# Attention, SoLU block and routed experts in one kernel: which queue issues the puts of p, the order of the last chunk's blocks, and the slots of three tails

## The chip, the cores and the metric

The kernel runs on one core of a Trainium2 chip (trn2). The metric is device microseconds for one execution. The kernel before takes 4489.14 us, the median of 3 runs (4488.82 to 4499.24).

## What is computed

Eight sequences of 3072 rows go through a squared-ReLU attention without softmax (its scores are `z zᵀ`, which is symmetric), then a SoLU block with a layer norm, then eight routed experts, one for each row. All matrix products are made at more than one pass' precision: each operand is split into a high and a low part, and three products are added.

```python
def _attn_ref(u, v, z):                      # u, v: (8, 3072, 256), z: (8, 3072, 64)
    scores = np.matmul(z, z.transpose(0, 2, 1)) / S
    attn = np.maximum(scores, 0.0) ** 2
    return u * np.matmul(attn, v)
def _moe_ref(x, w_in, w_out, g_ln):          # w_in: (256, 1024), w_out: (1024, 256)
    h = x @ w_in
    sm = softmax(h); solu = h * sm
    ln = (solu - mean(solu)) / sqrt(var(solu) + 1e-6) * g_ln
    return ln @ w_out
def _moe2_ref(x, w_gate, w1, w2):            # w1: (8, 256, 1024), w2: (8, 1024, 256)
    e = argmax(x @ w_gate); gate = softmax(x @ w_gate)[e]
    return gate * (np.maximum(x @ w1[e], 0.0) @ w2[e])
```

## The kernel before

**Chunks and slots.** The 24576 rows are cut into 48 chunks of 512 rows, six to a sequence; `c` counts chunks and j = c mod 6 is the place in the sequence. A chunk takes 24 slots, one for each block of 128 key rows. In a slot TensorE (PE) multiplies one block of squared scores `a`, split into `ah` and `al`, with that block's rows of v (`pe_av`: L108, L109, L110, two rounds of three matmuls into `o`). The order of everything is written out by hand: a loop over slots (L1044) emits for each slot the matmuls, what stands in a table of events (`at(slot, function, ...)`), and the steps of blocks that come up to seven slots later. Each engine and each queue runs its own list in this order, and nothing overtakes.

**Kept scores.** Since the scores are symmetric, a block that was made in an earlier chunk of the sequence is not made again. It is written to HBM (`put_out`, L399, `kept<-sym`) and read back (`get`, L406, `sym<-kept`, four transfers of 64 KB in runs of 128 bytes). `get` is emitted seven slots ahead of the block's own matmuls. Three slots behind `get` a block from four or more places back is transposed on VectorE (`turn_got`, L412); four slots behind it the block is split, the high part on ScalarE (`dve_hi`, L438), the low part a slot later on VectorE (`dve_lo`, L443). A chunk with j = 0, 1, 2, 3, 4, 5 reads 0, 4, 8, 12, 16, 16 of its 24 blocks; the rest needs two more matmuls (L422, L423) and two activations each. Only j up to 3 writes any.

**The tail of a chunk.** The 512 rows of chunk c then go through the SoLU block in four pieces t of 128 rows, six slots apart, while the slots of the next chunk run. For piece t the slot w = 24(c+1) + 2 + 6t counts: `blk_h` (PE), `blk_max` (DVE), `blk_exp` (ACT), `blk_mul` (DVE), at w + 4 `blk_turn` (a transposition on DVE into `pb`), at w + 5 `blk_put` (four transfers of 128 KB to HBM, `moved<-pb`, L536), later `blk_get` (four transfers back, `pT<-moved`, L542), `blk_split` (ACT and DVE) and `blk_y` (PE, then DVE into `y`). The four slot offsets of put, get, split and y are the tuple of L954. After the last piece come the scaling and the routing (mostly GpSimd, POOL) and four scatters of the rows into `sorted_rows` (`blk_scatter`, L659), one every two slots.

**Queues.** All transfers but the scatters are issued by SyncE's queue (SP), except that `blk_put` is issued by ScalarE's queue where its slot lies in a chunk with j = 4 or 5 and the tail is not the last one:

```python
at(w + out_, blk_put, c, t, nc.scalar if (w + out_) // NKB % NCB >= NCB - 2 and not last else nc.sync)
```

The program counts the transfers of SP and ScalarE on eight semaphores in turn (DMAHW0 to 7 in the rows of the order below), so that a transfer that comes to a semaphore is issued only after the transfer before it on that semaphore, eight back, has landed.

**The experts.** From slot NS = 1152 on, the sorted rows are taken in units of 512 rows (the first three in halves of 256), two matrix products each (`up`, `down`), while the tails of the chunks 45, 46 and 47 still run: their last scatters stand at NS + 8 to NS + 14, NS + 29 to NS + 35 and later. `load_x` (L805) reads a unit's rows out of `sorted_rows`; unit 2's stands at NS + 10. The tile `y` that a tail writes and its scatters read has two buffers, so chunk 47 writes the one that chunk 45 scattered from.

Of the kernel before, what the change touches and what calls it, by code (L numbers as in the profile page):

```python
# [33 lines left out]
def attention_moe_kernel(ctx, tc, u, v, z, w_in, w_out, g_ln, w_gate, w1, w2, out):  # L34
    nc = tc.nc
# [8 lines left out]
    NCB = S // CH  # L44
    NKB = S // P
    NCHUNK = B * NCB
# [6 lines left out]
    PD = 1  # L53
    ZL = 8
    XA, XT0, XE = 2, 21, 23
    SA, SB, SC, SD, SH = 11, 14, 16, 19, 1
    TW = 8
    WS, W0, W1, W2 = 4, -11, 0, 2
    YT = 1
# [72 lines left out]
    with ExitStack() as st:  # L132
# [22 lines left out]
        def at(slot, fn, *args):  # L155
            events[slot].append((fn, args))

        def after_them(slot, fn, *args):

            events_after[slot].append((fn, args))  # L160
# [3 lines left out]
        t = vp.tile([P, 2, 4, D], F32R, tag="vw", name="raw64").bitcast(I32).rearrange("p a r d -> p (a r d)")  # L164
        raw64 = [t[:, i * 2 * CH:(i + 1) * 2 * CH].rearrange("p (f two) -> p f two", two=2) for i in range(2)]
        t = mp.tile([P, F], F32, tag="pT", name="cu64").bitcast(I32)
        c64, u64 = t[:, :CH], t[:, CH:]
        t = [mp.tile([P, CH], F32R, tag=k, name="t64").bitcast(F32) for k in ("pth0", "ptl0", "pth1", "ptl1")]
# [165 lines left out]
        def again(q, k):  # L334
            return q == NCB - 2 and k == NCB - 1
# [11 lines left out]
        t = [xrow.tile([P, KD * CH], F32, tag="x", name="sym") for _ in range(2)]  # L347
        t = [x[:, i * CH:(i + 1) * CH] for x in t for i in range(2)]
# [3 lines left out]
        def order(j, end=False):  # L352


            old = [kb for kb in range(4 * j) if end or not again(kb // 4, j)]
            new = [kb for kb in range(NKB) if kb not in old]
            return [kb for _, kb in sorted([((i + 0.5) / len(old), kb) for i, kb in enumerate(old)] +
                                           [((i + 0.5) / len(new), kb) for i, kb in enumerate(new)])]

        orders = [order(c % NCB, c == NCHUNK - 1) for c in range(NCHUNK)]  # L360

        def block(n):
# [167 lines left out]

        moved = [nc.dram_tensor(f"moved_{i}", (32, 4, F), F32, kind="Internal").ap() for i in range(4)]

        def blk_put(c, t, eng):
            w = pb_t.pop((c, t))
            for x in range(4):
                eng.dma_start(out=moved[t][:, x], in_=w[x * 32:(x + 1) * 32])  # L536

        def blk_get(c, t):
            pT_t[c, t] = w = mp.tile([P, F], F32, tag="pT", name="pT")
# [299 lines left out]
        for i in range(NU):  # L839
            w = HALF if i < N_CUT else units[i]  # L840
# [71 lines left out]
        for c in range(NCHUNK):  # L912
            b, j = divmod(c, NCB)
            s0 = c * NKB
            sb = b * NCB * NKB
            if b == 0:
                base = 4 * j - Z0
                zload = base - 5 + (j > 0)
                vload = 4 * j - V0
                at(base, turn_z, c)  # L920
            else:

                late = j >= NCB - 2
                base = sb + 3 + 4 * (j - NCB + 2) if late else sb - (NCB - 1 - j) * NKB + ZB
                zload = base - (4 if late else ZL)
                vload = sb - NKB + VL + VS * j
                at(base - 2, turn_z, c)
            at(zload, load_z, c)
            at(base, prep_z, c)
            if c > 0:  # L930
                at(s0 - LA - 5, swap_z, c)
            for h in range(2):
                step, wait = (3, 5) if b else (2, 2)
                at(vload + step * h, load_v, c, h)
                at(vload + step * h + wait, prep_v, c, h)
                at(vload + step * h + wait + (b > 0), prep_v_lo, c, h)
            for x in range(4):
                at(s0 + 2 + x, load_u, c, x)
            at(s0 + 14, turn_u, c)

            last = c == NCHUNK - 1
            more = 2 if last else 1
            s1 = s0 + NKB
            for t in range(4):
                w = s1 + 2 + (TW if last else 6) * t
                at(w, blk_h, c, t, 0)
                at(w + 1, blk_h, c, t, 1)
                at(w + 1, blk_max, c, t)
                after_them(w + 2, blk_exp, c, t)
                at(w + 3, blk_mul, c, t)  # L950
                at(w + 4, blk_turn, c, t)
                at(w + 6, blk_var, c, t)

                out_, back, cut_, y = (4, 6, 10, 12) if last else (5, 8, 12, 15) if c < NCHUNK - 2 else (5, 7, 9, 12)  # L954

                at(w + out_, blk_put, c, t, nc.scalar if (w + out_) // NKB % NCB >= NCB - 2 and not last else nc.sync)
                at(w + back, blk_get, c, t)
                cut_, y = w + cut_, w + y
                at(cut_, blk_split, c, t, 0)
                at(cut_ + 1, blk_split, c, t, 1)  # L960
                at(y, blk_y, c, t, 0)
                at(y + 1, blk_y, c, t, 1)
            e = y + 3
            for i in range(3):
                at(e + more * i, blk_scale, c, i)
            for i in range(2):
                at(e + more * (3 + i), blk_scale, c, 3)
            at(e + more * 5, blk_logits, c)
            for i in range(10):
                at(e + more * (6 + i + 2 * (i > 5)), blk_route, c, i)  # L970
            for t in range(4):
                at(e + more * (6 + 2 * t), blk_rows, c, t)
                at(e + more * (18 + 2 * t), blk_scatter, c, t)
        after = e + more * 24
        for b in range(n_in + n_out):
            for i in range(14):
# [15 lines left out]
        s0 = NS - NKB  # L992
        at(s0, take, "raw1")
        at(s0, load_w, 0, 1)
        at(s0 + 5, take, "w1h")
        at(s0 + 10, take, "w1l")
        at(s0 + 14, take, "raw2")
        at(s0 + 14, load_w, 0, 2)
        at(s0 + 19, take, "xT0")
        at(NS, take, "w2h")  # L1000
        at(NS, take, "hT")
        at(NS, take, "w2l")
# [40 lines left out]
        with tc.manual_schedule():  # L1043
            for n in range(min(lo_slot, -LA), hi_slot + 1):  # L1044
                i = n + LA
# [62 lines left out]
```

## Time and profile before

| | us |
|---|---|
| median of 3 runs (lowest, highest) | 4489.14 (4488.82, 4499.24) |
| the profiled execution, its own time | 4495.23 |
| its span, first to last instruction | 4493.5 |
| PE busy in the span | 4293.5 (96%) |
| DVE, ACT, POOL busy | 3200.8, 2797.7, 1123.2 |
| granted TensorE clock, mean over the span | 0.981 |

The profiled execution lies 6.1 us above the median, and 1.7 us of its time lie outside of its span. The share of 96% is a mean over chunks that differ; the rows below take it apart by chunk.

### The profile page before, as it was taken

The numbers are of one execution on the slowest core, as the hardware profiler recorded it, in microseconds if no ns is written. First come the engines' busy times: TensorE is split into PE (matmuls) and PEld (weight loads), VectorE is DVE, ScalarE is ACT, GpSimd is POOL, SyncE is SP. The second block draws the span as 40 slices with busy tenths as digits, with TensorE's granted clock in tenths as the row PEclk, the third lists the DMA queues.
The fourth block names the chain that finished last, engine by engine and source line by source line (L and its number), as shares of the span: only waits on it lengthen the run. The fifth ranks groups of instructions, "written<-read, shape, count | busy, mean of one in ns | idle before, by whom it ended". The sixth has DMA issues, their size and how long they took to land. (4 is left out here: it accounts for less than half of the span.)

```text
span 4493.5 us, 74098 instructions
## 1 busy us (share of the span) xinstructions
PE 4293.5 (96%) x23458; PEld 3701.0 (82%) x23458; DVE 3200.8 (71%) x5624; ACT 2797.7 (62%) x5184; POOL 1123.2 (25%) x2358
## 2 busy tenths in 40 slices
PE   7999998999899999999999999999789999999998
PEld 5877887888788788878877887887678999999998
DVE  8767776777687677768767776777556755666686
ACT  6756775776577577658756765875444444444565
POOL 5022222322222232222223222322122211111112
PEclk9999999999999999999999999999889999999999
DMA  5887787778778778877887887778665655555575
GB/s 151 172 154 150 182 177 137 173 175 164 140 188 176 141 177 175 162 145 181 170 151 173 171 169 143 176 168 157 119 143 141 162 141 141 141 141 142 154 214 164
DMA packets 2529034, 719.20 MB, mean 160 GB/s; under 512 B 2326653, under 2 KB 2417021, under 8 KB 2528640
## 3 DMA queue, kind: packets, MB, share of 16 engines
q1 hardware_dynamic: 2497248, 629.76, 66.7%
q0 software_dynamic: 19104, 51.15, 3.3%
q10 hardware_dynamic: 12288, 33.57, 2.8%
q8 instruction: 183, 3.00, 0.3%
q14 instruction: 211, 1.73, 0.1%
HBM read 442.46 MB, written 273.49 MB: 159 GB/s over the span
## 5 line engine op out<-in xcount | busy, mean ns | idle before, releaser
L109 PE MATMUL o<-al,vw 128*128 128x512 f32 x2304 | 931.8, 404 | 136.9 <-DVE al L443 136.4
L108 PE MATMUL o<-ah,vw 128*128 128x512 f32 x2304 | 922.6, 400 | 4.5 <-DVE ut L467 4.4
L110 PE MATMUL o<-ah,vw 128*128 128x512 f32 x2304 | 915.1, 397 | 0.0
L438 ACT ACTIVATE ah<-a 128x512 fp32r<-128x512 f32 x832 | 525.6, 632 | 199.0 <-DVE a L412 95.2
L109 PEld LDWEIGHTS o<-al,vw 128*128 128x128 f32 x2304 | 442.8, 192 | 250.8 <-DVE al L443 172.6
L428 ACT ACTIVATE r<-s 128x512 f32<-128x512 f32 x704 | 414.6, 589 | 376.8 <-PE s L423 359.3
L433 ACT ACTIVATE a<-r 128x512 f32<-128x512 f32 x704 | 438.5, 623 | 238.2 <-issue 101.6
L443 DVE TENSOR_TENSOR al<-a,ah 128x512 fp32r<-128x512 f32 x832 | 577.5, 695 | 1.2 <-ACT ah L438 0.3
L110 PEld LDWEIGHTS o<-ah,vw 128*128 128x128 f32 x2304 | 443.3, 192 | 94.4
L108 PEld LDWEIGHTS o<-ah,vw 128*128 128x128 f32 x2304 | 441.6, 192 | 91.2 <-DVE ut L467 5.9
L105 DVE TENSOR_TENSOR ptl<-pT,pth 128x512 fp32r<-128x512 f32 x384 | 264.9, 690 | 328.3 <-ACT pth L104 327.2
L108 PE MATMUL yp<-gw,pth 128*128 128x264 f32 x1536 | 445.0, 290 | 0.4 <-ACT pth L104 0.4
L109 PE MATMUL yp<-gw,pth 128*128 128x264 f32 x1536 | 443.9, 289 | 0.0
L110 PE MATMUL yp<-gw,ptl 128*128 128x264 f32 x1536 | 442.9, 288 | 0.2 <-DVE ptl L105 0.2
L865 ACT ACTIVATE zw_x<-g 128x512 fp32r<-128x512 f32 (+1 forms) x350 | 182.6, 522 | 402.9 <-PE g L110 392.4
L866 DVE SCALAR_TENSOR_TENSOR zw_x<-g,zw_x 128x512 fp32r<-128x512 f32 (+1 forms) x350 | 208.2, 595 | 266.5 <-ACT zw_x L865 261.3
L108 PEld LDWEIGHTS yp<-gw,pth 128*128 128x128 f32 x1536 | 296.3, 193 | 16.6 <-ACT pth L104 0.6
L109 PEld LDWEIGHTS yp<-gw,pth 128*128 128x128 f32 x1536 | 296.6, 193 | 15.6
L659 POOL DMA_INDIRECT sorted_rows<-y,pi x192 | 205.6, 1071 | 402.6 <-DMA sorted_rows<-y,pi 330.8
L491 PE MATMUL h<-w_in,xt 128*128 128x512 f32 x768 | 305.5, 398 | 0.0
L490 PE MATMUL h<-w_in,xt 128*128 128x512 f32 x768 | 305.3, 398 | 0.0
L110 PEld LDWEIGHTS yp<-gw,ptl 128*128 128x128 f32 x1536 | 296.0, 193 | 0.6 <-DVE ptl L105 0.6
(275 smaller groups left out, 10520.7 us busy)
## 6 DMA issues: line engine op xcount, KB each, us to landing
vw_x<-in_moe_w SPq DMA_DIRECT2D x124, 1024.0 KB
sym<-kept SPq DMA_DIRECT2D x1792, 64.0 KB
pT<-moved SPq DMA_DIRECT2D x768, 128.0 KB
kept<-sym SPq DMA_DIRECT2D x320, 256.0 KB
moved<-pb SPq DMA_DIRECT2D x512, 128.0 KB
kept<-a SPq DMA_DIRECT2D x128, 256.0 KB
moved<-pb ACTq DMA_DIRECT2D x256, 128.0 KB
vr<-in_v SPq DMA_DIRECT2D x96, 256.0 KB
```

The costliest lines, as they stand in the source:

```text
L105: V.tensor_tensor(out=lo, in0=src, in1=hi.bitcast(F32), op=ALU.subtract)
L108: T.matmul(out=out, lhsT=lh, rhs=rh, start=start, stop=False, **kw)
L109: T.matmul(out=out, lhsT=lh, rhs=rl, start=False, stop=False, **kw)
L110: T.matmul(out=out, lhsT=ll, rhs=rh, start=False, stop=stop, **kw)
L428: A.activation(out=r, in_=s_t.pop(n), func=AF.Relu)
L433: A.activation(out=a, in_=r_t.pop(n), func=AF.Square)
L438: A.activation(out=h, in_=a_t[n], func=AF.Copy)
L443: V.tensor_tensor(out=l, in0=a_t[n], in1=ah_t[n].bitcast(F32), op=ALU.subtract)
L490: T.matmul(out=h[:, fs], lhsT=w[:, 0, kd, ts_], rhs=w_in_t[0][:, kd, fs], start=(kd == 0), stop=False)
L491: T.matmul(out=h[:, fs], lhsT=w[:, 0, kd, ts_], rhs=w_in_t[1][:, kd, fs], start=False, stop=False)
L659: G.indirect_dma_start(out=xs[:DUMMY], out_offset=bass.IndirectOffsetOnAxis(ap=pi[:, t:t + 1].bitcast(U32), axis=0), in_=y_t[c][:, t, :], ...
L866: V.scalar_tensor_tensor(out=lo, in0=h, scalar=0.0, in1=hi.bitcast(F32), op0=ALU.max, op1=ALU.subtract)
```

## The change

Four things are changed. (1) `blk_put` is issued by SP everywhere. (2) The last chunk (c = 47) orders its blocks in another way: the 16 kept ones are spread over the first 20 slots among the four of k = 4, and its own four blocks (kb 20 to 23) come last; before, 20 blocks (16 kept, then the four of k = 4) were spread over all 24 slots among its own four, so that the kept ones took 19. The slots at which the first expert's buffers are taken and its weights split move by one or two with it. (3) The tuple of offsets (put, get, split, y) goes from (5, 8, 12, 15) to (5, 7, 10, 12) for c = 45, and from (5, 7, 9, 12) to (5, 7, 10, 12) for c = 46; all that follows a tail's y, routing and scatters, comes three slots earlier for c = 45. (4) The four scatters of c = 45 and 46 stand one slot apart in place of two.

```diff
-    SA, SB, SC, SD, SH = 11, 14, 16, 19, 1
+    SA, SB, SC, SD, SH = 12, 15, 17, 19, 1
...
-            old = [kb for kb in range(4 * j) if end or not again(kb // 4, j)]
+            old = [kb for kb in range(4 * j) if not again(kb // 4, j)]
             new = [kb for kb in range(NKB) if kb not in old]
+            rest = new[len(new) - 4 * end:]
+            new = new[:len(new) - 4 * end]
             return [kb for _, kb in sorted([((i + 0.5) / len(old), kb) for i, kb in enumerate(old)] +
-                                           [((i + 0.5) / len(new), kb) for i, kb in enumerate(new)])]
+                                           [((i + 0.5) / len(new), kb) for i, kb in enumerate(new)])] + rest
...
-        def blk_put(c, t, eng):
+        def blk_put(c, t):
             w = pb_t.pop((c, t))
             for x in range(4):
-                eng.dma_start(out=moved[t][:, x], in_=w[x * 32:(x + 1) * 32])
+                nc.sync.dma_start(out=moved[t][:, x], in_=w[x * 32:(x + 1) * 32])
...
-                out_, back, cut_, y = (4, 6, 10, 12) if last else (5, 8, 12, 15) if c < NCHUNK - 2 else (5, 7, 9, 12)
-
-                at(w + out_, blk_put, c, t, nc.scalar if (w + out_) // NKB % NCB >= NCB - 2 and not last else nc.sync)
+                out_, back, cut_, y = (4, 6, 10, 12) if last else (5, 8, 12, 15) if c < NCHUNK - 3 else (5, 7, 10, 12)
+                at(w + out_, blk_put, c, t)
...
-                at(e + more * (18 + 2 * t), blk_scatter, c, t)
+                at(e + more * (18 + t * (1 if NCHUNK - 4 < c and not last else 2)), blk_scatter, c, t)
...
-        at(s0 + 5, take, "w1h")
-        at(s0 + 10, take, "w1l")
-        at(s0 + 14, take, "raw2")
-        at(s0 + 14, load_w, 0, 2)
-        at(s0 + 19, take, "xT0")
+        at(s0 + 6, take, "w1h")
+        at(s0 + 11, take, "w1l")
+        at(s0 + 16, take, "raw2")
+        at(s0 + 16, load_w, 0, 2)
+        at(s0 + 21, take, "xT0")
```

How the puts move, at one place: the end of chunk 45 (j = 3) and the start of chunk 46 (j = 4), where the fourth piece of chunk 44 is put (`moved_3`). The list of SP before, each transfer with the semaphores that it waits for:

```order
L542 DMA pT_35812<-moved_2 32x32x32 [waits DMAHW3_49,DVE_49]
L542 DMA pT_35812<-moved_2 32x32x32 [waits DMAHW4_49]
L542 DMA pT_35812<-moved_2 32x32x32 [waits DMAHW6_49]
L542 DMA pT_35812<-moved_2 32x32x32 [waits DMAHW1_49]
L399 DMA kept_1_5_3<-sym_150 128x512 [waits DMAHW3_49,DVE_49]
L406 DMA sym0_151<-kept_1_4_0 32x16x32 [waits DMAHW4_49]
L406 DMA sym0_151<-kept_1_4_0 32x16x32 [waits DMAHW5_49]
L406 DMA sym0_151<-kept_1_4_0 32x16x32 [waits DMAHW6_49]
L406 DMA sym0_151<-kept_1_4_0 32x16x32 [waits DMAHW7_49]
```

The same place in the list of ScalarE before; the puts hold the semaphores 5, 7, 0 and 2 that SP's list leaves out:

```order
L428 ACTIVATE r_35909<-s_35879 128x512
L438 ACTIVATE ah_35911<-a_35864 128x512
L536 DMA moved_3<-pb_35899 32x1024 x4
L433 ACTIVATE a_35935<-r_35909 128x512
L438 ACTIVATE ah_35937<-a_35935 128x512
L104 ACTIVATE pth0_35946<-pT_35812 128x512
```

And the list of SP of the change (from L360 on its lines stand two higher):

```order
L544 DMA pT_35812<-moved_2 32x32x32 x4
L401 DMA kept_1_5_3<-sym_150 128x512
L408 DMA sym0_151<-kept_1_4_0 32x16x32 x4
L408 DMA sym1_152<-kept_1_4_1 32x16x32 x4
L538 DMA moved_3<-pb_35899 32x1024 x4
L408 DMA sym2_153<-kept_1_4_1 32x16x32 x4
L328 DMA ur_35958<-in_u 32x16x32 x2
L408 DMA sym3_154<-kept_1_4_1 32x16x32 x4
```

Before, the second transfer of `sym0_151` stands on semaphore 5 behind the first put, which is in the list of another engine and one and a half reads further on in the order of slots. In the change the same put stands in SP's own list, behind the whole of `sym0_151` and `sym1_152`.

How the scatters move: POOL's list at the start of the experts. The first `sorted_rows` rows are chunk 45's scatters, the rows `vv` and `tt` are the scaling of chunk 46's tail, `out_y` the finished rows of the first expert unit. Before:

```order
L655 CAST pi<-pf 128x4
L659 DMA sorted_rows<-y,pi 198656x264
L907 DMA out_y<-a_x,ids 24576x256 x2
L659 DMA sorted_rows<-y,pi 198656x264
L576 TENSOR_SCALAR vv<-se 128x4
L577 TENSOR_TENSOR vv<-vv 128x4
L578 TENSOR_SCALAR vv<-vv 128x4
L579 TENSOR_TENSOR vv<-vv,q 128x4
L580 TENSOR_SCALAR vv<-vv 128x4
L659 DMA sorted_rows<-y,pi 198656x264 x2
```

In the change:

```order
L657 CAST pi<-pf 128x4
L661 DMA sorted_rows<-y,pi 198656x264 x4
L909 DMA out_y<-a_x,ids 24576x256 x2
L578 TENSOR_SCALAR vv<-se 128x4
L579 TENSOR_TENSOR vv<-vv 128x4
L580 TENSOR_SCALAR vv<-vv 128x4
L581 TENSOR_TENSOR vv<-vv,q 128x4
L582 TENSOR_SCALAR vv<-vv 128x4
```

The four scatters now stand together, ahead of the first finished rows, at NS + 5 to NS + 8; unit 2's `load_x` at NS + 10, which before stood among them, comes after all four.

## Rows read from the trace of the kernel before

**Rows 1.** The page: busy time of each engine, and the issues of puts by the two queues.

```profile
PE 4293.5 (96%) x23458; PEld 3701.0 (82%) x23458; DVE 3200.8 (71%) x5624; ACT 2797.7 (62%) x5184; POOL 1123.2 (25%) x2358
...
moved<-pb SPq DMA_DIRECT2D x512, 128.0 KB
...
moved<-pb ACTq DMA_DIRECT2D x256, 128.0 KB
```

**Rows 2.** Busy time by window: the chunks with j = 2, 3, 4 and 5 of the third sequence (c = 14 to 17), each from its first `o` matmul to the next chunk's. Columns: length, then PE, PEld, DVE, ACT, POOL busy with the number of instructions, granted clock, DMA share, GB/s.

```profile
960.50:1023.40 62.90, 62.90 (x322) 53.41 (x321) 51.12 (x89) 45.26 (x83) 16.41 (x42) 1.00 0.80 167
1023.40:1084.90 61.50, 61.50 (x316) 52.24 (x315) 49.89 (x87) 41.88 (x77) 15.56 (x42) 1.00 0.90 178
1084.90:1155.50 70.60, 62.85 (x308) 51.48 (x307) 43.15 (x76) 37.09 (x67) 17.42 (x42) 0.98 0.80 140
1155.50:1229.50 74.00, 65.67 (x314) 53.53 (x312) 48.26 (x83) 40.53 (x72) 21.30 (x48) 0.95 0.74 143
```

**Rows 3.** The same view, first the sum over seven windows, each j = 4 and 5 of one of the first seven sequences (its first number is the length of all 14 chunks); then the eighth sequence's j = 4 (c = 46) and j = 5 (c = 47).

```profile
sum 1012.60, PE 907.06 PEld 744.24 DVE 639.25 ACT 542.86 POOL 269.85; mean PE 129.58 PEld 106.32 DVE 91.32 ACT 77.55 POOL 38.55
...
3083.50:3154.60 71.10, 63.93 (x308) 52.47 (x306) 49.31 (x120) 36.04 (x65) 17.15 (x42) 0.95 0.78 136
3154.60:3243.30 88.70, 68.00 (x305) 55.21 (x305) 45.99 (x80) 38.72 (x70) 15.88 (x39) 0.88 0.70 126
```

**Rows 4.** Waits over the whole span: who waited for whom, total us, times, longest us. The first row is PE's longest, the others SP's.

```profile
PE o L109 <- DVE al L443: 136.4, 72, 9.7
...
SPq L536 <- DVE pb L527: 299.2, 87, 17.1
SPq L406 <- DMA moved<-pb: 170.1, 51, 7.5
```

**Rows 5.** Timeline of the first stall of c = 46, by engine (SP, ACT, DVE, PE): start, us, engine and line, what, count, and in brackets the idle time before it with what ended it. Equal rows that follow each other are merged.

```profile
3080.90 13.75 SPq L406 DMA_DIRECT2D sym<-kept  x12
...
3086.70 1.73 ACTq L536 DMA_DIRECT2D moved<-pb  x4
3088.48 0.63 ACT L433 ACTIVATE a<-r 128x512 f32<-128x512 f32 x1 [4.19 <-issue]
...
3085.43 1.23 DVE L527 STREAM_TRANSPOSE pb<-p 128x1024 f32<-128x1024 f32 x1
...
3092.21 0.71 DVE L412 STREAM_TRANSPOSE a<-sym 128x512 f32<-128x512 f32 x1 [4.88 <-DMA sym<-kept]
...
3093.55 0.79 PE L109 MATMUL o<-al,vw 128*128 128x512 f32 x1 [2.16 <-DVE al L443]
```

**Rows 6.** SP's waits (the queue's own) in three of the windows of rows 2: the longest of j = 3, then those of j = 4 that are over 2 us, then those of j = 5 over 2 us.

```profile
SPq L399 <- DVE al L443: 1.1, 3, 0.4
...
SPq L399 <- DMA moved<-pb: 6.4, 1, 6.4
SPq L406 <- DMA moved<-pb: 5.9, 3, 3.0
SPq L328 <- DMA moved<-pb: 4.5, 1, 4.5
...
SPq L406 <- DMA moved<-pb: 13.2, 4, 6.6
SPq L328 <- DMA moved<-pb: 3.6, 1, 3.6
SPq L542 <- DVE ptl L105: 3.0, 1, 3.0
```

**Rows 7.** Timeline of SP: a put by SP in c = 45 (j = 3), and runs of reads without a stop in c = 46 (j = 4).

```profile
3070.15 1.78 SPq L536 DMA_DIRECT2D moved<-pb  x4
...
3111.12 6.64 SPq L406 DMA_DIRECT2D sym<-kept  x12
```

**Rows 8.** Waits in the window of c = 47: PE's longest and SP's two longest; then a row of ACT's timeline there.

```profile
PE o L109 <- DVE al L443: 20.4, 6, 9.7
...
SPq L406 <- DMA moved<-pb: 14.8, 4, 5.7
SPq L542 <- DMA moved<-pb: 10.3, 1, 10.3
...
3206.66 0.63 ACT L104 ACTIVATE pth<-pT 128x512 fp32r<-128x512 f32 x1 [6.32 <-DMA pT<-moved]
```

**Rows 9.** Timeline at the start of the experts (which begin at 3243.3): POOL's scatters of chunk 45, SP's `load_x` of unit 2, DVE and PE, and the window behind PE's wait with its clock (columns as in rows 2).

```profile
3273.15 1.07 POOL L659 DMA_INDIRECT sorted_rows<-y,pi  x1 [0.89 <-POOL pi L655]
3284.95 0.98 POOL L659 DMA_INDIRECT sorted_rows<-y,pi  x1 [0.30 <-issue]
3295.19 1.08 POOL L659 DMA_INDIRECT sorted_rows<-y,pi  x1 [7.80 <-DMA gi<-sorted_rows]
3301.44 0.98 POOL L659 DMA_INDIRECT sorted_rows<-y,pi  x1 [5.17 <-DMA sorted_rows<-y,pi]
...
3287.52 4.09 SPq L805 DMA_DIRECT2D x<-sorted_rows  x8
...
3305.58 0.49 DVE L565 SCALAR_TENSOR_TENSOR y<-gw_sum,nmp,yp 128x264 f32<-128x264 f32 x1 [11.94 <-issue]
...
3306.46 0.58 PE L108 MATMUL g<-vw_x,zd_x 128*128 128x256 f32 x1 [10.13 <-DVE zw_x L866]
...
3306.40:3312.00 5.60, 5.54 (x20) 4.96 (x21) 4.17 (x10) 1.73 (x4) 2.95 (x5) 0.50 0.63 202
```

## The prediction

> **What bounds the kernel now.** I read the page first: PE is busy for 96% of the span [rows 1], so on the mean there is little to win. That mean hides two kinds of chunk, which the windows by chunk show. At j = 2 and 3 PE is busy for the whole of the window at full clock: 62.9 and 61.5 us [rows 2]. Each step of j replaces four made blocks by read ones, so j = 4 and 5 have less PE work than j = 3, yet they take 70.6 and 74.0 us, with PE idle for some 8 us and the mean clock at 0.98 and 0.95 [rows 2]. It is the same in every sequence: the 14 such chunks of the first seven take 1012.6 us, 72.3 each [rows 3]. So the loss sits in 16 of 48 chunks, and these are the ones whose puts ScalarE issues: 256 of 768 transfers [rows 1].
>
> Then the waits. PE's one long wait is for `al`, the low part made by DVE: 136.4 us in 72 pieces [rows 4]. Who is late behind DVE is seen in the first stall of c = 46 [rows 5], read from its end. PE waits 2.16 us for `al`; DVE had waited 4.88 us for a kept block to arrive from HBM; that block's read stands among SP's 12 transfers, which took 13.75 us, where 12 in a row take 6.64 [rows 7], so SP stood still for 7.1 us. SP's waits name what it stood for: landing of `moved<-pb`, in j = 4 6.4 + 5.9 + 4.5 = 16.8 us, in j = 5 13.2 + 3.6 = 16.8 us; in j = 3, where SP issues the puts itself, its largest total is 1.1 us [rows 6].
>
> The rows of the order ahead tell why: the puts hold semaphores of the common eight, so SP's read that comes eight transfers later waits for a put in the list of ScalarE, and that put waits for its place there (the put's slot is later than the read's) and for `pb` from DVE. A read that is needed soon is tied to a put that comes later.
>
> **Part 1, the puts.** Replay of that stall in the new order. SP reaches the stop after one transfer of `sym0`, at about 3081.4. In the change the other three and the four of `sym1` follow at once: 7 × 0.553 us (6.64/12 [rows 7]) = 3.9, so 3085.3. Then the put waits for `pb`, which DVE finishes at 3085.43 + 1.23 = 3086.66 [rows 5]: 1.3 us. Its four issues take 1.78 us [rows 7], and SP goes on at 3088.4. Before, it stood until about 3088.6 (3080.90 + 13.75 less 11 issues of 0.553 [rows 5, 7]), with those seven reads still to issue. So SP is 3.9 us further, and the block that DVE got at 3092.21 is there some 7 us earlier: the stall is gone.
>
> Does SP have the time? Each chunk gets 16 more issues on SP, 4 × 1.78 = 7.1 us. In j = 4 SP then needs 70.6 − 16.8 + 7.1 = 60.9 us; in j = 5, without the 3.0 us behind `ptl` as well, which it spends because it is early, 74.0 − 19.8 + 7.1 = 61.3 [rows 2, 6, 7]. The nearest row for a chunk with a full SP queue and its own puts is j = 3: 61.5 us, no PE idle, SP waiting for next to nothing [rows 2, 6]. I take 61.5 for j = 4 and for j = 5. Bounds: PE's own need is another 1.4 us lower (the step from j = 2 to 3 [rows 2]), 60.1; the upper one is the first rival's. Over the first seven sequences this gives 14 × 61.5 = 861.0 against 1012.6: −151.6. For c = 46, 71.1 → 61.5: −9.6 [rows 3]. The clock comes back with the idle time; its loss is inside these windows and not counted again.
>
> ScalarE loses 4.19 us less at each put [rows 5]. It is busy for 37 to 41 of 71 to 74 us [rows 2], so this is worth nothing by itself. The mean DMA share is 0.80 and 0.74 in j = 4 and 5 and 0.90 in j = 3 [rows 2], so the same bytes in 61.5 us (0.80 × 70.6/61.5 = 0.92) ask little more than j = 3 does already without a stall.
>
> The Trainium skill (DMA: Bandwidth & Descriptors, Issuing engines are not separate DMA queues) has a rule that speaks against this part: issuing from several engines saves the sequencer's issue time, and nothing else. By it alone the change only hands 64 puts of 1.78 us back to SP, which would be 114 us lost if SP is the limit. The rows agree on the price (1.73 us on ScalarE, 1.78 on SP), but they also show the wait for landing, which the rule leaves out.
>
> **Part 2, the last chunk.** c = 47 takes 88.7 us at clock 0.88 [rows 3]; PE waits 20.4 us, SP stands 14.8 + 10.3 = 25.1 us for puts, and ACT waits up to 6.32 us for `pT`, whose read sits behind such a put [rows 8]. SP also loads the first expert here, so it stays the limit: 88.7 − 25.1 + 7.1 = 70.7 us, −18.0. The other order spreads 16 reads over 20 slots in place of 19, one slot more for `pT` before its split in c = 46 takes some of ACT's wait: both lie inside this term. The moved takes and the later second weight load have slots to spare before NS and cost nothing; if that cover failed, they'd cost a slot or two, under 6 us.
>
> **Part 3, shorter tail and denser scatters.** At the start of the experts PE waits 10.13 us, behind DVE, which stands 11.94 us at `y` (L565): chunk 47's first `y` needs the buffer from which chunk 45 scatters, and the fourth scatter is issued only at 3301.44 [rows 9]. The four are strung out because unit 2's `load_x` stands among them: it waits for two scatters (issued at 3287.52, behind the one of 3284.95), and the third waits 7.80 us for its reads. In the change all four go three or more slots earlier, ahead of that `load_x`. The wait goes: −10.1, and the 5.6 us behind it at clock 0.50 [rows 9] would take half: −2.8. Together −12.9. What is late next is `load_x` itself, if the fourth scatter is; scatters follow each other by 6.2 us at worst here (3295.19 to 3301.44), so the wait could at most come back as a part of the 10. Bounds 0 and −20.
>
> **Sum.** −151.6 − 9.6 − 18.0 − 12.9 = −192.1. The profiled execution took 4495.2 by its own time, so 4303.1; it lies 6.1 above the median, so 4297 in the terms of the runs.
>
> **Rivals.**
> First, SP becomes the limit: the puts wait for `pb` at every piece, as in the replay (1.3 us), or the reads come slower in a fuller queue. If each of the four puts costs as much again as its issues, j = 4 and 5 take 61.5 + 7.1 = 68.6 us; 15 × 7.1 = 107 of the gain is lost, some 5 more in c = 47: about 4409. For it: 60.9 of 61.5 us leaves no slack. Against: j = 3 runs so. A read is issued seven slots ahead of its use and must be there when DVE turns it, three slots later, 7.7 us; 2.2 for the issues and about 1.9 for the landing (3090.3 to 3092.21 in the stall above) leave 3.6 us by which SP may lag, and DVE is up to two slots ahead of PE.
>
> Second, slower: the stop stays as long as it was, since the put waits for the same `pb`, and SP pays 7.1 us more in each of the 16 chunks: +114, less 12.9 of part 3: about 4590. For it: SP's waits for `pb` now, 299.2 us in 87 pieces, 3.4 each [rows 4]. It decides where a put stops SP, beyond what it can catch up, for over (70.6 − 60.9)/4 = 2.4 us. Against: these pieces lie in chunks where SP has time left; in j = 3, with a full queue, none shows above 1.1 us in total [rows 6].
>
> Third, no change: the reads are late because of the DMA engines, not of the puts, and only part 3 pays: about 4476. Against: the DMA share of 0.90 in j = 3 without a stall.
>
> **Chances.** The forecast 0.60 (its own range 4262 to 4335: at the low end every chunk of j = 4 and 5 at 60.1, −21, and c = 47 and part 3 better by 14; at the high end 2.5 us more in each of the 15 chunks), the first rival 0.27 (4335 to 4440), the third 0.06, the second 0.07. A difference of 0.3%, 13 us, is about what a measurement of this kernel can tell from none. The third rival lies on that bound; half of it counts as no change, as does a small part of the first and second: faster 0.88, same 0.05, slower 0.07. Range 4262 to 4410.
>
> **What would show it.** Right: windows of j = 4 and 5 at 60 to 63 us with PE busy throughout and clock 1.00; no wait of SP for `moved<-pb` over a few us in total; PE's wait for `al` under 30 us; c = 47 near 71; the 11.94 us at `y` gone. Wrong: SP rows for `pb` (L538 in the changed kernel) over 10 us in a chunk of j = 4 or 5, DVE or ACT still waiting there for `sym<-kept`, or `load_x` waiting for the fourth scatter with PE behind it.

## The result, and the profile after

The changed kernel takes 4353.3 us (median), the kernel before 4489.5 in the same comparison: a ratio of 0.969, 95% interval 0.967 to 0.971. It is 136 us faster, where 192 were forecast: 4353.3 lies 56 us above the 4297 that were named, and inside the range of 4262 to 4410. The profiled execution took 4350.7 by its own time, 144.6 less than the one before; the terms below are compared with that difference. Times of kernels are medians of their executions; one execution of the first of the two last kernels took 6950.9 us at a granted clock of 0.56, a slow run, and its median is that of the other three.

The page after, PE's busy time and the puts (line numbers from L360 on are two higher than before):

```profile
PE 4240.6 (98%) x23458; PEld 3667.5 (84%) x23458; DVE 3198.7 (74%) x5624; ACT 2798.8 (64%) x5184; POOL 1123.0 (26%) x2358
...
moved<-pb SPq DMA_DIRECT2D x768, 128.0 KB
```

PE executes the same instructions and is busy for 53 us less [rows 1], although the span ends 145 us sooner: the same matmuls show as longer where the granted clock is lower (an `o` matmul of the `al` round 404 ns on the mean before, 397 after), and the mean clock rose from 0.981 to 0.994 as the idle time went, as the forecast had it.

The windows after, for j = 2 to 5 of the third sequence, then c = 46 and c = 47 (columns as in [rows 2]), and, from the same view over seven windows, the sum over the 14 chunks with j = 4 and 5 of the first seven sequences:

```profile
926.30:989.10 62.80, 62.80 (x322) 53.31 (x321) 51.03 (x88) 45.17 (x83) 15.63 (x42) 1.00 0.79 167
989.10:1050.70 61.60, 61.60 (x317) 52.34 (x316) 50.13 (x87) 41.98 (x77) 15.24 (x42) 1.00 0.90 179
1050.70:1112.30 61.60, 60.07 (x308) 50.52 (x307) 43.36 (x76) 37.08 (x67) 16.20 (x42) 1.00 0.89 156
1112.30:1178.10 65.80, 62.56 (x314) 51.56 (x312) 47.63 (x83) 40.81 (x72) 22.74 (x48) 1.00 0.90 164
2965.20:3031.60 66.40, 61.64 (x308) 51.41 (x306) 49.26 (x120) 36.03 (x66) 17.91 (x42) 0.97 0.86 144
3031.60:3110.70 79.10, 65.25 (x305) 53.23 (x305) 47.11 (x84) 37.27 (x68) 15.80 (x46) 0.91 0.75 142
...
sum 894.00, PE 860.98 PEld 716.67 DVE 637.65 ACT 545.43 POOL 268.95; mean PE 123.00 PEld 102.38 DVE 91.09 ACT 77.92 POOL 38.42
```

j = 2 and 3 are what they were [rows 2]. The 14 chunks fell from 1012.6 to 894.0 us, -118.6 [rows 3]; j = 4 is nearly as short as forecast (61.6 here, 62.2 on the mean of seven), j = 5 is not (65.8 here, 65.5 on the mean). c = 46 lost 4.7 us, c = 47 9.6 [rows 3]. From the first matmul of the experts to the end it was 1250.2 us and is now 1238.4: -11.8. Together -144.7.

The waits after, PE's two longest, then two of SP's:

```profile
PE o L109 <- DVE al L445: 47.4, 43, 3.8
PE yp L108 <- ACT pth L104: 19.5, 5, 8.0
...
SPq L538 <- DVE pb L529: 300.0, 89, 13.3
...
SPq L544 <- DMA moved<-pb: 21.0, 30, 1.8
```

PE's wait for `al` went from 136.4 to 47.4 us [rows 4]; 43 short pieces are left. SP's wait for the landing of `moved<-pb` at reads of kept blocks, 170.1 us [rows 4], is no longer among SP's waits at all; the 21.0 us at L544 (20.6 before, in the same view) is the read of `pT`, which has to wait for its own put. SP's wait for `pb` is 300.0 as it was 299.2, so the second rival's price was not paid: those waits lie where SP has time. In j = 4 and 5 SP hardly waits, and yet PE does. The longest stall of c = 17 (j = 5) shows for what (timeline of SP, DVE and PE):

```profile
1126.05 2.73 SPq L544 DMA_DIRECT2D pT<-moved  x4
...
1128.83 1.31 SPq L328 DMA_DIRECT2D ur<-in_u  x2
...
1130.23 0.43 SPq L305 DMA_DIRECT2D vr<-in_v  x1
1130.72 2.10 SPq L408 DMA_DIRECT2D sym<-kept  x4
...
1132.86 1.30 SPq L328 DMA_DIRECT2D ur<-in_u  x2
1134.21 2.35 SPq L408 DMA_DIRECT2D sym<-kept  x4
...
1136.35 0.71 DVE L414 STREAM_TRANSPOSE a<-sym 128x512 f32<-128x512 f32 x1 [5.71 <-DMA sym<-kept]
...
1137.68 0.50 PE L109 MATMUL o<-al,vw 128*128 128x512 f32 x1 [1.70 <-DVE al L445]
```

From 1126.05 on SP issues one transfer after the other without a stop; the block that DVE waits 5.71 us for is read at 1130.72, behind four reads of `pT`, two loads of `u` and one of `v`. SP does not stand there: it gets to that read late. The landing is slow too: the last of the four issues ends at 1132.82 and DVE starts at 1136.35, 3.5 us later, where the prediction had allowed 1.9. Both are the first rival's mechanism, at part of its price.

### The profile page after: what moved, and what is told of

Same layout as the page of the kernel before. It is cut to its first block, busy times and chain, and to the rows that moved or that the text cites. A ratio compares the mean times of both kernels' runs of the same rounds, so it can differ in the third digit from the quotient of the medians.

```text
span 4348.9 us, 74270 instructions
## 1 busy us (share of the span) xinstructions
PE 4240.6 (98%) x23458; PEld 3667.5 (84%) x23458; DVE 3198.7 (74%) x5624; ACT 2798.8 (64%) x5184; POOL 1123.0 (26%) x2358
## 4 chain that ended last, share of the span: by engine, by line
PE 69%; SPq 10%; DMA 8%; DVE 7%; issue 3%; ACT 2%; POOL 0%; DVEq 0%; POOLq 0%; ACTq 0%
PE o L109 8%; PE o L108 8%; PE o L110 8%; SPq L408 5%; PE y L108 3%; PE y L109 3%; PE y L110 3%; PE g L108 3%; PE g L109 3%; PE g L110 3%; PE yp L108 3%; PE yp L110 3%; PE yp L109 3%; PE s L424 3%; PE s L425 3%; PE h L492 3%
## 5 line engine op out<-in xcount | busy, mean ns | idle before, releaser
L109 PE MATMUL o<-al,vw 128*128 128x512 f32 x2304 | 914.4, 397 | 47.8 <-DVE al L445 47.4
L108 PE MATMUL o<-ah,vw 128*128 128x512 f32 x2304 | 911.2, 395 | 3.2 <-DVE ut L469 2.7
L110 PE MATMUL o<-ah,vw 128*128 128x512 f32 x2304 | 901.6, 391 | 0.0
L440 ACT ACTIVATE ah<-a 128x512 fp32r<-128x512 f32 x832 | 525.8, 632 | 189.9 <-issue 63.9
L110 PEld LDWEIGHTS o<-ah,vw 128*128 128x128 f32 x2304 | 435.1, 189 | 93.6
L108 PEld LDWEIGHTS o<-ah,vw 128*128 128x128 f32 x2304 | 435.1, 189 | 88.4 <-issue 4.0
L108 PE MATMUL yp<-gw,pth 128*128 128x264 f32 x1536 | 440.3, 287 | 19.5 <-ACT pth L104 19.5
L109 PE MATMUL yp<-gw,pth 128*128 128x264 f32 x1536 | 439.0, 286 | 0.0
L104 ACT ACTIVATE pth<-pT 128x512 fp32r<-128x512 f32 x384 | 237.7, 619 | 146.5 <-DMA pT<-moved 146.3
L108 PEld LDWEIGHTS yp<-gw,pth 128*128 128x128 f32 x1536 | 290.2, 189 | 36.3 <-ACT pth L104 21.5
L109 PEld LDWEIGHTS yp<-gw,pth 128*128 128x128 f32 x1536 | 291.1, 190 | 14.5
```

Source lines behind the costliest of these rows:

```text
L104: A.activation(out=hi, in_=src, func=AF.Copy)
L108: T.matmul(out=out, lhsT=lh, rhs=rh, start=start, stop=False, **kw)
L109: T.matmul(out=out, lhsT=lh, rhs=rl, start=False, stop=False, **kw)
L110: T.matmul(out=out, lhsT=ll, rhs=rh, start=False, stop=stop, **kw)
L440: A.activation(out=h, in_=a_t[n], func=AF.Copy)
```

## The experiments

### Which part of the change did it

The first kernel is the kernel before, with the puts on SP and nothing else.

```
-  at(w + out_, blk_put, c, t, nc.scalar if (w + out_) // NKB % NCB >= NCB - 2 and not last else nc.sync)
+  at(w + out_, blk_put, c, t, nc.sync)
```

> The kernel before with one edit: all puts of p are issued by SP (the change's first part alone). By the forecast's terms it takes 151.6 + 9.6 us off the kernel before, about 4328. By the windows of the changed kernel, where the 14 chunks of j = 4 and 5 fell by 118.7 us and c = 46 by 4.8, about 4366. If SP only stops for the same time in another place (the second rival) it is slower, about 4600; if the DMA engines were the cause (the third rival), within 0.3% of 4489.

It took 4367.1 us, ratio 0.973 (0.971 to 0.975): -124.3, and its 14 chunks add up to 894.6 us, as in the changed kernel (first row below). The second is the complement, the changed kernel with that line as it was before.

> The changed kernel with its puts of j = 4 and 5 back on ScalarE: the order of the last chunk, the tails and the scatters alone. By the forecast 12.9 us below the kernel before, 4476, with the 14 chunks of j = 4 and 5 again near 72.3 us each. If the last chunk's shorter window (79.1 for 88.7 us) comes from its order and not from the puts, some 10 us less still, 4466. If the parts need one another, no faster than 4489.

It took 4477.1 us, ratio 0.997 (0.996 to 0.998), -14.3; its 14 chunks are back at 1006.0 (second row).

```profile
sum 894.60, PE 862.67 PEld 717.95 DVE 640.37 ACT 545.30 POOL 269.13; mean PE 123.24 PEld 102.56 DVE 91.48 ACT 77.90 POOL 38.45
...
sum 1006.00, PE 900.69 PEld 738.69 DVE 639.42 ACT 544.51 POOL 273.22; mean PE 128.67 PEld 105.53 DVE 91.35 ACT 77.79 POOL 39.03
```

The two add up to -138.6, against -136 for both at once: the parts don't need one another, and nine tenths of the gain is the issuing engine of 64 puts (256 transfers). Their last two chunks (first kernel, then second; c = 46 and 47 in each):

```profile
2966.10:3030.00 63.90, 60.13 (x307) 50.13 (x306) 48.88 (x120) 36.02 (x65) 16.49 (x42) 1.00 0.85 147
3030.00:3115.00 85.00, 65.75 (x305) 53.16 (x305) 46.07 (x80) 38.58 (x70) 15.35 (x39) 0.90 0.74 134
```

```profile
3078.80:3150.70 71.90, 63.97 (x308) 52.38 (x306) 48.89 (x120) 36.00 (x66) 16.50 (x42) 0.95 0.79 133
3150.70:3234.40 83.70, 67.00 (x305) 53.04 (x305) 47.54 (x84) 37.66 (x68) 15.85 (x46) 0.88 0.72 134
```

In c = 47 (88.7 before) the puts alone give 3.7 us and the order with its tail 5.0, both 9.6. In c = 46 the puts alone reach 63.9, and the changed kernel has 66.4: something in the other parts costs there.

### Is it the late put that stops SP

The removed mechanism was put where it never was: the puts that fall into j = 3 go to ScalarE, those of j = 4 and 5 stay on SP.

```
-  at(w + out_, blk_put, c, t)
+  at(w + out_, blk_put, c, t, nc.scalar if (w + out_) // NKB % NCB == NCB - 3 else nc.sync)
```

> The changed kernel, with the puts that fall into j = 3 on ScalarE (j = 4 and 5 stay on SP): the removed mechanism put where it never was. If the cause before was a put that is late in ScalarE's list and holds SP's reads by the shared semaphores, j = 3 grows from 61.5 to about 70 us as j = 4 had it, 8 x 8.5 = 68 us: about 4420. If what cost was only the number of reads in j = 4 and 5, j = 3 stays at 61.5: 4353; and if SP's saved issues counted most, j = 3 would gain nothing, PE being its limit.

It took 4458.2 us, ratio 0.993, 105 above the changed kernel. A window of j = 3 (61.6 there), and SP's waits in it:

```profile
1411.00:1485.90 74.90, 65.82 (x316) 54.67 (x315) 49.18 (x87) 41.60 (x77) 16.24 (x42) 0.95 0.73 144
```

```profile
SPq L544 <- DMA moved<-pb: 19.1, 3, 7.9
SPq L408 <- DMA moved<-pb: 4.4, 1, 4.4
```

SP has 16 issues fewer and the chunk is 12.4 us longer on the mean of seven. So j = 4 and 5 lost their time to the put in ScalarE's list, and not to their many reads. One thing was not as expected: here SP stands 19.1 us at the read of `pT`, which needs the put's data, and only 4.4 us at a kept block that shares its semaphore. In the kernel before it was the shared semaphore, at lines that do not touch `moved` [rows 6]. Either way the late put holds all that is behind it in SP's list.

These two kernels leave one rival. ScalarE stands still behind its puts as well (4.19 us in [rows 5]; 101.6 us in 27 pieces before an `a` over the whole span of the kernel before), and that came and went together with SP's stops. The trace of the kernel before tells the two apart. In its 14 chunks PE pauses for 102.6 us, in 62 pieces of over 0.15 us. Followed back from each of them, at each step to what released it, 101.5 us in 60 pieces lead to a transfer that SP issued late after a stop for the landing of a put, at a line that does not touch `moved`. With the puts of j = 3 on ScalarE, 53.6 of the 58.4 us of seven chunks lead to a stop for a put, most at reads of `pT`. So ScalarE's own stop is at most a small part.

### Is SP's issue time what is left

The dose: each put of j = 4 as eight transfers of 64 KB in place of four of 128, 16 issues more on SP for the same bytes.

```
-  for x in range(4):
-      nc.sync.dma_start(out=moved[t][:, x], in_=w[x * 32:(x + 1) * 32])
+  r = 32 // n
+  for x in range(4 * n):
+      j = x % n * r
+      nc.sync.dma_start(out=moved[t][j:j + r, x // n], in_=w[x * r:(x + 1) * r])
...
-  at(w + out_, blk_put, c, t)
+  at(w + out_, blk_put, c, t, 2 if (w + out_) // NKB % NCB == NCB - 2 else 1)
```

> The changed kernel, with each put of j = 4 as eight transfers of 64 KB in place of four of 128 KB: the same bytes, 16 issues more on SP in such a chunk, by about 0.4 us each some 6.5 us. If SP has no time left in j = 4, the eight windows grow by nearly all of that, 62.2 to about 68 us: about 4400. If SP has slack (the nearest row of the forecast, j = 3 without a stall) they grow by under 2 us: below 4370.

It took 4411.1 us, 58 more than the changed kernel. Seven chunks with j = 4 grew from 435.2 to 485.4 us, 7.2 each, which is 16 x 0.45; j = 5 stayed at 458.4 (458.7). A window of j = 4:

```profile
1455.70:1524.50 68.80, 62.29 (x308) 52.00 (x307) 43.43 (x76) 37.38 (x67) 16.67 (x42) 0.98 0.84 139
```

The whole price of the added issues is in the window, and the DMA share fell from 0.89 to 0.84: SP has no slack in j = 4, and the DMA engines, less busy than before, are not what it waits for. The opposite dose: the eight loads of `u` of each chunk with j = 5 are issued by GpSimd.

```
-  nc.sync.dma_start(out=u_raw[c][x * 32:(x + 1) * 32, k].rearrange("i (a j) -> i a j", j=32), in_=src[k, x])
+  (nc.gpsimd if c % NCB == NCB - 1 else nc.sync).dma_start(out=u_raw[c][x * 32:(x + 1) * 32, k].rearrange("i (a j) -> i a j", j=32), in_=src[k, x])
```

> The changed kernel, with the 8 loads of u in every chunk of j = 5 issued by GpSimd in place of SP: 8 x 0.5 = 4 us less of SP's time there, nothing else in j = 4. If SP's issue time is what j = 5 lacks, its windows fall from 65.5 to about 62 us, 7 x 3.5 = 25 us: about 4329, with j = 4 unchanged at 62.2. If the DMA engines are the limit, 4353 as it is; if GpSimd's own issues hold up its scatters, slower.

It took 4339.7 us, ratio 0.967 (0.966 to 0.969), -13.6 to the changed kernel. j = 4 and j = 5 of one sequence:

```profile
1429.10:1491.30 62.20, 60.47 (x308) 50.53 (x307) 43.43 (x76) 37.13 (x67) 16.86 (x42) 1.00 0.87 156
1491.30:1554.90 63.60, 62.22 (x313) 51.63 (x313) 47.18 (x83) 40.71 (x73) 27.09 (x56) 1.00 0.99 168
```

j = 4 is unchanged, seven chunks with j = 5 fell from 458.7 to 448.0 us: 1.5 each, where 3.5 were expected, with 2.9 more in c = 47. The sign is right and the size is not: counted from SP's rows, the other 94 issues of such a chunk became dearer (57.0 us for 94, where the changed kernel has 58.0 for 102), so that less time came free than 8 x 0.5 us. Why they did is open.

The decisive one takes the puts of j = 4 and 5 off SP without giving them to ScalarE: GpSimd issues them.

```
-  at(w + out_, blk_put, c, t)
+  at(w + out_, blk_put, c, t, nc.gpsimd if (w + out_) // NKB % NCB >= NCB - 2 and not last else nc.sync)
```

> The changed kernel, with the puts of j = 4 and 5 issued by GpSimd, neither by ScalarE (before) nor by SP (after). If SP's own time is what is left to win (16 issues, 7.1 us of a chunk's), PE is the limit again: the windows fall to PE's busy time at full clock in the changed kernel, 60.4 for 62.2 us in j = 4 and 62.5 for 65.5 in j = 5, 7 x 4.8 = 34 us, about 4320. If any queue other than SP's is late with its puts and stops SP's reads by that, as ScalarE's did, the windows go back to 71 to 73 us: about 4480. If the DMA engines are the limit: 4353.

It took 4301.2 us, ratio 0.958 (0.957 to 0.960), 52 below the changed kernel. The windows of j = 3, 4 and 5 of one sequence, and the issues of its puts by GpSimd:

```profile
1352.20:1413.70 61.50, 61.50 (x316) 52.24 (x315) 49.85 (x87) 42.00 (x77) 15.30 (x42) 1.00 0.89 177
1413.70:1473.50 59.80, 59.80 (x309) 50.85 (x308) 44.65 (x77) 37.79 (x68) 24.91 (x58) 1.00 1.00 170
1473.50:1534.70 61.20, 61.20 (x314) 51.77 (x314) 49.45 (x84) 41.31 (x74) 28.58 (x64) 1.00 0.96 175
```

```profile
moved<-pb POOLq DMA_DIRECT2D x256, 128.0 KB
```

PE is busy from the first to the last of each window. The 14 chunks take 853.5 us:

```profile
sum 853.50, PE 849.04 PEld 717.35 DVE 653.83 ACT 551.86 POOL 378.67; mean PE 121.29 PEld 102.48 DVE 93.40 ACT 78.84 POOL 54.09
```

That is 421.6 for j = 4 and 431.9 for j = 5, 60.2 and 61.7 each, and with 849.0 us of it busy nearly what PE needs by itself. The 894.0 - 853.5 = 40.5 us between is what the 16 issues a chunk still cost on SP in the changed kernel. Slower landing does not explain it: from the start of its issue a kept block's transfer lands here after 3.0 us in j = 4 and 3.5 in j = 5 (medians over the seven sequences), later than in the changed kernel with 2.6 and 3.1, and PE does not wait. The DMA share reaches 1.00 without a wait of PE, so the DMA engines are not the limit in the changed kernel at 0.90. And it is not any second queue that hurts. GpSimd's puts are counted on eight semaphores of their own, none of SP's waits at a kept block names a put in this kernel, and in the windows of j = 4 and 5 shown SP stops behind one only at a read of `pT` (4.0 us). Where GpSimd's puts are late they do stop SP: for 14.3 us at reads of `pT` in c = 47 of the same kernel. Whether ScalarE's puts would have cost less on semaphores of their own was not tried.

### Fewer, larger puts

Two kernels tried to save SP's issues by larger transfers: each put as one of 512 KB, and later as two of 256 KB.

```
-  for x in range(4):
-      nc.sync.dma_start(out=moved[t][:, x], in_=w[x * 32:(x + 1) * 32])
+  nc.sync.dma_start(out=moved[t].rearrange("j x f -> x j f"), in_=w)
```

> The changed kernel, with each put as one transfer of 512 KB in place of four of 128 KB: 12 issues fewer on SP in a chunk, 12 x 0.45 = 5.4 us, the same bytes. If SP's own issue time is what j = 4 and 5 lack (first rival), j = 5 falls from 65.5 to about 62 us and j = 4 from 62.2 to about 61, together 7 x 4.7 = 33 us, and the last two chunks give some 5: about 4315. If the reads are late because the DMA engines are slow to serve them, the same 4353.

It took 5188.7 us, ratio 1.157 (1.155 to 1.160): far slower. The issues, one put with the four reads behind it (SP's timeline), and a window in which that put was under way:

```profile
moved<-pb SPq DMA_DIRECT2D x192, 512.0 KB
```

```profile
1222.50 0.57 SPq L537 DMA_DIRECT2D moved<-pb  x1
1223.12 7.10 SPq L408 DMA_DIRECT2D sym<-kept  x4
```

```profile
1224.00:1231.00 7.00, 7.00 (x35) 5.61 (x34) 5.33 (x9) 5.33 (x10) 0.62 (x1) 1.00 0.38 85
```

The issue is as cheap as hoped, 0.57 us for a whole put. But a put lands 10.0 us (median of 192) after the end of its issue, where one of the four lands in 1.8, and the reads that come behind it land with it: the four took 7.10 us to issue, and the DMA share is 0.38. Counted over the trace's packets of 4 KB, four were under way at once for half of the time in which any was, and more for 0.15 of it; in the changed kernel it is 14 to 17 for half of that time. The Trainium skill (DMA: Bandwidth & Descriptors, Why a DMA increments its semaphore by 16 and not by 1) states the reason: a transfer runs on the largest number of DMA engines, 16 at most, that divides the slowest dimension of both sides. Here that dimension has 4 steps on the side of `moved`. By this rule two transfers of 64 partitions, whose slowest dimension has 2 steps, get two engines each:

> The changed kernel, with each put as two transfers of 256 KB (64 partitions each; the outer dimension of the destination has 2 steps, with 32 rows of 4 KB in each). In the kernel with one transfer of 512 KB (outer dimension 4) at most about four packets of 4 KB were under way at a time and the put took 10.5 us to land; with four transfers of 32 rows it is 16 and 1.6 to 2 us. If the outer dimension sets how many DMA engines a transfer is spread over, each of these gets two: a put lands in about 10 us and the kernel stays near 5190 us. If the size or the number of partitions did it, landing takes some 5 us at most and, with 8 issues fewer on SP, the time is between 4320 and 4600.

It took 5971.7 us, ratio 1.329, worse still. Two packets of 4 KB were under way for 0.69 of the time in which any was, a transfer lands after 11.7 us (median of 384), and DVE's transposes into `pb` now wait for the puts before them:

```profile
L529 DVE STREAM_TRANSPOSE pb<-p 128x1024 f32<-128x1024 f32 x192 | 238.6, 1243 | 531.1 <-DMA moved<-pb 531.1
```

The rule and the traces agree: mostly 14 to 17, 4 and 2 packets at a time for 32, 4 and 2 steps. The expectation for the single transfer had left the rule out.

### The tail and the scatters

At the start of the experts after: DVE's `y`, which had waited 11.94 us [rows 9], a late `pth` (the high part of `pT`) with PE behind it, and the window at the lower clock there.

```profile
3121.02 0.49 DVE L567 SCALAR_TENSOR_TENSOR y<-gw_sum,nmp,yp 128x264 f32<-128x264 f32 x1 [0.52 <-PE yp L110]
...
3135.27 0.59 PE L108 MATMUL yp<-gw,pth 128*128 128x264 f32 x1 [5.71 <-ACT pth L104]
```

```profile
3132.50:3139.30 6.80, 4.01 (x15) 3.48 (x16) 3.11 (x5) 2.55 (x6) 1.95 (x2) 0.50 0.87 225
```

The wait at `y` is gone, and a shorter one of another kind, for a `pT` that SP read late, stands there with its own stretch at clock 0.50. Two kernels undo one half of the third part each. First the tail of chunk 45:

```
-  (5, 8, 12, 15) if c < NCHUNK - 3 else (5, 7, 10, 12)
+  (5, 8, 12, 15) if c < NCHUNK - 2 else (5, 7, 10, 12)
```

> The changed kernel, with the tail of chunk 45 as it was (offsets 5, 8, 12, 15); chunk 46 keeps 5, 7, 10, 12 and the scatters stay one slot apart. If the shorter tail makes pT late, c = 46 falls from 66.3 us to the 63.9 that it has with the puts alone. What chunk 45's three slots give at the start of the experts is then lost: by the forecast up to the 12.9 us of the whole third part, by half of its six slots about 6. Together 4345 to 4363, no difference if the two are alike.

It took 4360.9 us, 7.6 above the changed kernel. From the first matmul of the experts to the end it takes 1251.2 us, so all of the 11.8 is lost again; c = 46 and 47 get

```profile
2967.70:3029.70 62.00, 60.20 (x307) 50.09 (x305) 47.97 (x119) 36.51 (x66) 16.77 (x42) 1.00 0.85 148
3029.70:3110.60 80.90, 65.05 (x305) 52.88 (x305) 47.24 (x80) 37.62 (x68) 17.24 (x40) 0.92 0.78 143
```

c = 46 falls from 66.4 to 62.0: the shorter tail costs 4.4 us there, since `pT` comes too late for its split (PE waits 2.7 us for `pth` in c = 46 of the changed kernel, and not here). Then the scatters, two slots apart again:

```
-  at(e + more * (18 + t * (1 if NCHUNK - 4 < c and not last else 2)), blk_scatter, c, t)
+  at(e + more * (18 + t * 2), blk_scatter, c, t)
```

> The changed kernel, with the four scatters two slots apart again; the shorter tails stay. With the tail of chunk 45 undone instead, the time from the start of the experts to the end was back at 1251.0 us, against 1238.2 in the changed kernel and 1250.2 before. If the fourth scatter's place alone decides, undoing its three slots here costs as much: 1250, about 4365. If the tail alone did it and the spacing is idle, 1238 and 4353.

It took 4352.6 us, no difference, with 1241.1 us from the experts on. The tail did it; the closer scatters are worth 2.7 us at most, about as much as that stretch differs between kernels that are alike in it.

### Better than both

Two last kernels start from GpSimd's puts, give GpSimd the loads of `u` of c = 47, and let chunk 46 split and multiply one slot later (5, 7, 11, 13). In the second, the puts issued in c = 47 are SP's.

```
-  at(w + out_, blk_put, c, t, nc.gpsimd if (w + out_) // NKB % NCB >= NCB - 2 and not last else nc.sync)
+  at(w + out_, blk_put, c, t, nc.gpsimd if (w + out_) // NKB % NCB >= NCB - 2 and c < NCHUNK - 2 else nc.sync)
```

The first of them:

> The kernel with GpSimd's puts (4301 us), and in the last chunks: the 8 loads of u of c = 47 on GpSimd, and chunk 46's tail with the split and the product one slot later (5, 7, 11, 13). If c = 47 lacks SP's time, it falls from 78.1 by about the 2.9 us that the loads of u gave there, and the slot more for pT takes 2 to 5 us of the 8.4 that PE waits for its split: 4293 to 4298. If the later tail delays the experts, no gain: 4301.

The second, with the line above:

> As the one before, with the puts of chunk 46 (those issued in c = 47) on SP: GpSimd has the scatters there too, and its puts land late, SP standing 14.3 us for them. If that stop is what holds c = 47, it is a few us faster than with all puts on GpSimd, about 4290; if SP's 16 issues weigh more, slower by up to 7.

They took 4291.4 us, ratio 0.956 (0.954 to 0.958), and 4296.4 us, 0.956 (0.955 to 0.958): no difference clear of noise, so it matters little who issues the puts of c = 47. That chunk, in the first of the two:

```profile
2983.00:3053.60 70.60, 64.37 (x306) 52.76 (x307) 47.80 (x86) 37.39 (x68) 30.53 (x70) 0.93 0.88 159
```

Against GpSimd's puts alone, c = 47 went from 78.1 to 70.6 us, and PE's wait for `pth` there from 8.4 to 0.2. This is the fastest kernel of the study, 62 us below the changed one. Which of its three steps gave how much in c = 47 was not separated.

## Why the prediction was right, and where its sizes failed

**The cause was right.** The 14 chunks lost their time because SP's reads stopped behind puts that were late in ScalarE's list: taken away it gives 124 us by itself, set up in j = 3 it costs 12.4 us a chunk, and the pauses of PE lead back to it. Signs named for it came true: j = 4 at 60 to 63 us, clock 1.00, the 11.94 us at `y` gone, and no stop of SP for `moved` at kept blocks (what is left for `moved`, 21.0 us, lies at reads of `pT`). Others did not: PE's wait for `al` did not fall under 30 us, j = 5 missed its 60 to 63 and c = 47 its 71. And a sign that had been named for being wrong is there: DVE still waits for `sym<-kept` in j = 5, 5.71 us in the stall above.

**Part 1 was forecast at -151.6 and gave -118.6.** The step that failed is "does SP have the time". It took SP's need from the windows before, less its waits and plus 16 issues: 60.9 and 61.3 us, just inside 61.5. Two things were wrong with it. The issues were priced as SP had made them while it stood still in between. On the mean of seven chunks with j = 5, 85 issues took 46.9 us before; after, the 86 that are not puts took 50.5. Single issues of over 1 us became more frequent, 30 in the seven chunks where there had been 19; why is open. With the puts 58.0 us of issues, 5.1 us between them and 2.0 of stops, 1.7 of these at the read of `pT`, SP's list of j = 5 is as long as the window, 65 us. And a list that is full on the mean is late wherever its transfers come in a cluster (`pT`, `u`, `v` ahead of a read, as in the timeline above); the 3.6 us by which SP was allowed to lag did not cover that, and had been worked out with a landing of 1.9 us where that stall shows 3.5. j = 3 was the nearest row, but it has no stall with 60.6 us of issues and the time between them; j = 4 and 5 have 62.0 and 63.1 in the changed kernel (means of seven).

**PE's own need was nearly right.** 61.5 us for each stood on j = 3; the kernel with GpSimd's puts shows 60.2 and 61.7. That j = 5 does not go below j = 3 could be seen in the trace before, which has the same counts: PE makes eleven score blocks in it and eight in j = 4, since the first of the next sequence are made there (rows of PE's `s` in c = 16, then in c = 17, after):

```profile
L424 PE MATMUL s<-zw 128*128 128x512 f32 x8 | 3.1, 389 | 0.0
```

```profile
L424 PE MATMUL s<-zw 128*128 128x512 f32 x11 | 4.3, 389 | 0.0
```

So "each step of j replaces four made blocks by read ones" held up to j = 4 only. It changed the sum little: 861.0 was forecast, 853.5 is reached when GpSimd issues the puts.

**c = 46 was forecast at -9.6 and gave -4.7**, for a reason that was not in the sum: the third part's shorter tail, costed at nothing there, makes `pT` late and takes 4.4 us of it back.

**c = 47 was forecast at 70.7 us and took 79.1.** The sum let SP's waits go and put nothing in their place. SP still stands 6.7 us for one `pb`, and it issues a read of `pT` late in a list that also has the rows for the first expert; the `pth` made of it comes 3.3 us after the last of the four issues, and PE waits 8.04 us (SP, ACT and PE in c = 47):

```profile
3072.26 2.11 SPq L408 DMA_DIRECT2D sym<-kept  x4
3074.47 3.00 SPq L544 DMA_DIRECT2D pT<-moved  x4
...
3080.79 0.63 ACT L104 ACTIVATE pth<-pT 128x512 fp32r<-128x512 f32 x1 [7.95 <-DMA pT<-moved]
...
3081.47 0.59 PE L108 MATMUL yp<-gw,pth 128*128 128x264 f32 x1 [8.04 <-ACT pth L104]
```

The kernel that takes the puts and the loads of `u` off SP there and gives `pT` a slot more reaches 70.6 us: the size was that of a kernel in which SP has the time.

**Part 3 was forecast at -12.9 and gave -11.8**, by the named wait, but half of its reason is idle: the tail moves the scatters early enough, their spacing does not matter.

**The rivals.** The second did not happen: SP's waits for `pb` did not grow. The third would have left about 13 us in all; the puts alone gave 124. The first came true in its mechanism (slower reads in a fuller queue; not the puts' wait for `pb`: SP's waits at puts come to 0.8 us in j = 5 of the third sequence and to none in j = 4), at 40 us where its full price was 107.

By the rule of the Trainium skill (DMA: Bandwidth & Descriptors, Issuing engines are not separate DMA queues) that several issuing engines save the sequencer's time and nothing else, the puts alone should have cost time; they gained 124 us, so the rule leaves out the waits that a late transfer brings to another queue. The time that it does name is real, and not small here: it is what GpSimd's puts gain.

## What to carry to other kernels

A transfer issued from a second queue is late with everything ahead of it in that engine's list, and holds the first queue wherever that one waits for its landing, by data or by a shared semaphore; look whose landing an idle queue waits for before looking at bandwidth. When work is moved onto a queue, take its list from a stretch where it runs without a stop, add the moved issues, and ask of each cluster whether the read behind it still comes in time: full on the mean is late in places. If the queue is then the limit, a third engine with idle time and semaphores of its own can be better than both.

## What the runs showed of the hardware that was not expected

An issue of SP has no fixed price: in the changed kernel a put of 128 KB took 0.42 us (median), a transfer of a kept block 0.54 on the mean and single ones up to 2.1 us. What holds such an issue was not tried and stays open. GpSimd issued the same puts in 0.50 us each (median of 256), hardly more than SP, and they landed 2.8 us after the end of the issue, where SP's took 1.8. And one transfer of 512 KB whose slowest dimension has 4 steps lands 10 us after its issue, where four of 128 KB are all there some 3.6 us after the first issue begins (1.78 us for the four [rows 7], and 1.8 for the last to land).
